# LayerNorm 2 of the first 512 tokens moved into the recurrence, the last segment woven into the first FFN chunks, one tile for the gate/up tails, LayerNorm 1's statistics issued later, and an extra output projection of half as many matmuls, in an attention-recurrence plus gated-FFN kernel

## The chip, the cores and the metric

The kernel runs on one core of one Trainium2 chip. The metric is device microseconds of one launch, the median of several runs; lower is better. A single launch is also recorded by the hardware profiler, and all views below come from such profiled executions. Engine names in them are PE (TensorE matmul), PEld (TensorE weight load), DVE (VectorE), ACT (ScalarE), POOL (GpSimd) and SP (the queue that issues DMAs); "L557" is line 557 of the kernel's file.

## The reference, cut to what matters

The sequence has S = 2048 tokens of width D = 640. Attention runs over 64 segments of 32 tokens. Each segment also sees 8 memory tokens, which are the attention output of the segment before it at its memory rows, so the segments are a chain. Then comes a gated FFN of width F = 1728.

```python
def _A_ref(x, mem0, Wq, Wk, Wv, Wo, seg_len):      # H=32 heads of 128, M=8 memory tokens
    mem, outs = mem0, []
    for s in range(n_seg):                          # 64 segments, one after the other
        h = concat([mem, x[:, s*32:(s+1)*32]])      # 40 rows
        q, k, v = h @ Wq, h @ Wk, h @ Wv
        p = softmax(mask(q @ k.T * scale))
        o = einsum('bhte,hed->btd', p @ v, Wo)
        mem = o[:, :8]                              # goes into the next segment
        outs.append(o[:, 8:])
    return concat(outs)

h  = x + _A_ref(layernorm(x), ...)                  # LN1
h2 = h + (relu(n @ W_gate) * (n @ W_up)) @ W_down   # n = layernorm(h), which is LN2
```

## The kernel before: the parts that matter

The kernel is one list of operations with read and write keys; a small dependency solver turns the keys into semaphore waits, and each engine executes its own operations in the order in which they were added. That last point decides much below: a ScalarE or VectorE operation stands behind every operation that was added for that engine before it, whether it needs it or not (in the changed kernel ScalarE once stood idle for 4.76 us in this way, and moving an operation ahead gained 8 to 10 us; both are shown below).

TensorE computes for each segment the projections (`project`, L339 and L325), transposes, scores, the memory rows' p·v (`pv_mem`), their transposes (`trans_om`) and output projection (`wo_pass`, 32 head blocks times four column groups of 32 output partitions), then the other rows' p·v (`pv_x`, L557). VectorE and ScalarE evacuate PSUM in between. The memory path, from scores to the next segment's memory rows, is the chain.

In this kernel a pass takes 32 rows of a segment, 8 of memory and 24 tokens. The last 8 tokens of each of four segments are therefore gathered in `oTe` and get an extra output projection in one pass, 16 times in all. It stands in two halves in the segments with s mod 4 = 1:

```python
    def wo_pass(src, keys, bk, halves=(0, 1)):
        for hf in halves:
            def f(pe, hf=hf):
                for hb in range(16 * hf, 16 * hf + 16):
                    w = Wo[:, head(hb // 4, hb % 4), :].rearrange("p (c g j) -> p g c j", g=4, j=32)
                    for gg in range(4):              # four column groups, 160 columns each
                        i = pe.matmul(bank(bk)[32 * gg:32 * gg + 32, 0:160], src[:, hb, :], w[:, gg],
                                      start=(hb == 0), stop=(hb == 31), ...)
# ... cut ...
    for s in range(NSEG):
        # ... projections, transposes, scores, exp_mem, cut ...
        if s == NSEG - 2:                            # W gate and W up overwrite Wq's space
            dma(Wg, ..., w=[("W", 0, 0), ("W", 0, 1), ("Wg",)])
            dma(Wu, ..., w=[("W", 0, 0), ("W", 0, 1), ("Wu",)])
        if last:
            for i in range(2):
                ln2_front(i)                         # load x and attention, add, row statistics, scale
            dma(Wd, ...)
        if units: ev[0] = units[0](); ...            # first half of the extra pass, or other extras
        if not last: pv_mem(s)
        exp_x()
        if units: ev[1] = units[1](); ev[1]()        # second half; ScalarE copies it out
        if woe: woe_store(s // 4 - 1)
        if s % 4 == 1 and ln:
            ln1_front(nb, xt, ("xt",))               # LN1: statistics and scale of the next 128 rows
        if last:
            for i in range(2):
                ln2_back(i, BQ[i])                   # transpose into xn2T
                ln2_front(i + 2)
        if not last: trans_om(s)                     # TensorE, then the VectorE copy into oT
        if s >= 1: trans_ox(s - 1, T0)
        # ... cut ...
        wo_pass(oT[par], ...)                        # needs that copy
        to_act(s + 1, ...)                           # memory rows of the next segment
        # ... stores, cut ...
        pv_x(s)
        if fin: fin()                                # Q or K of 32 further tokens: ScalarE evacuates
```

The FFN then runs over four blocks of 512 tokens: 14 chunks of gate and up (13 of 128 columns and a tail of 64), then the down products. Each down group sums all 14 chunks, so it waits for the last product into `hT`.

Of the kernel before, what the change touches and what calls it, by code (L numbers as in the profile page):

```python
# [163 lines left out]
def build_kernel(nc, A_x, A_mem0, A_Wq, A_Wk, A_Wv, A_Wo, A_seg_len, B_W_gate, B_W_up, B_W_down, out):  # L164
# [19 lines left out]
    x_ap, out_ap, mem0_ap = A_x[0], out[0], A_mem0[0]  # L184
    attn_d = nc.dram_tensor("attn_d", [S, 4, DC * 32], BF16)
# [11 lines left out]
    Wg = ffn.alloc("Wg", [128, DC, F], BF16)  # L197
    Wu = ffn.alloc("Wu", [128, DC, F], BF16)
# [3 lines left out]
    xt2 = [ffn.alloc(f"xt2_{i}", [128, D], BF16) for i in range(2)]  # L202
    at = [ffn.alloc(f"at{i}", [128, D], BF16) for i in range(2)]
    h_rows = [[ffn.alloc(f"h0_{u}", [128, D], BF16) for u in range(4)]]
    g1 = [ffn.alloc(f"g1_{i}", [128, TB], BF16) for i in range(3)]
    osb = [ffn.alloc(f"osb{i}", [128, D], BF16) for i in range(3)]
    xn2T = [ffn.alloc("xn2T0", [128, DC, TB], BF16)]
    assert ffn.off <= 2 * DC * HD * 2
    ffn.off = 2 * DC * HD * 2
    h_rows.append([ffn.alloc(f"h1_{u}", [128, D], BF16) for u in range(4)])  # L210
# [26 lines left out]
    wtoke = ar.alloc("wtoke", [128, DC, 32], BF16)  # L237
    TBf = ar.alloc("TBf", [128, DC, 32], F32)
    xt = ar.alloc("xt", [128, D], BF16)
    st = ar.alloc("st", [128, 2, 6], F32)  # L240
# [61 lines left out]
    def norm_rows(src, skey, n, dst, dkey):  # L302
        for q in range(2):
            add("dve", lambda v, q=q: v.bn_stats(st[0:n, q, :], src[0:n, q * 320:(q + 1) * 320]), r=[skey],  # L304
                w=[("st", q)])
        add("dve", lambda v: v.bn_aggr(mv[0:n, :], st[0:n, :, :]), r=[("st", 0), ("st", 1)], w=[("mv",)])
        add("act", lambda a: a.activation(lv[0:n, :], mv[0:n, 1:2], ACTF.Ln, bias=eps[0:n, 0:1], scale=1.0),
            r=[("mv",), ("eps",)], w=[("lv",)])
        add("act", lambda a: a.activation(rs[0:n, :], lv[0:n, :], ACTF.Exp, scale=-0.5), r=[("lv",)], w=[("rs",)])
        add("dve", lambda v: v.tensor_scalar(dst[0:n, :], src[0:n, :], mv[0:n, 0:1], rs[0:n, 0:1], ALU.subtract,  # L310
                                             ALU.mult), r=[skey, ("mv",), ("rs",)], w=[dkey])
# [103 lines left out]
    def ln1_front(b, buf, key):  # L415
        t0, n = (0, 64) if b < 0 else (64 + 128 * b, min(128, S - 64 - 128 * b))
        norm_rows(buf, key, n, buf, key)
# [34 lines left out]
    def to_act(s, wkey, src):  # L452
# [4 lines left out]
            w=[("act", b % 2, j, "m")])  # L457

# [78 lines left out]

    def wo_rows(bk, dst, dkey, eng):
        copy_op(eng, dst[:].rearrange("p c j -> p (c j)"), bank(bk)[:, 0:160], [B(bk)], [dkey])
# [43 lines left out]
    def attn_keys(i):  # L583
        ks = []
        for s in range(4 * i, 4 * i + 4):
            ks += [("attn", 32 * s, g) for g in range(4)] + [("attn", 32 * s + RID, g) for g in range(4)]
        return ks

    def ln2_front(i):
        par, u, e = (i // 4) % 2, i % 4, i % 2  # L590
        x2, xk, a2, ak = xt2[e], ("xt2", e), at[e], ("at", e)
        dma(x2[:, :], x_ap[128 * i:128 * i + 128, :], r=[("Wdone", 1)], w=[xk])
        dma(a2[:, :], attn_d[128 * i:128 * i + 128, :, :].rearrange("t g f -> t (g f)"), r=attn_keys(i) + [("Wdone", 1)],
            w=[ak])
        h = h_rows[par][u]
        hk = ("h", par, u)
        add("dve", lambda v: v.tensor_tensor(ap(h, 0, [[128, 5], [32, 4], [1, 32]]),
                                             ap(x2, 0, [[128, 5], [32, 4], [1, 32]]),
                                             ap(a2, 0, [[32, 5], [160, 4], [1, 32]]), ALU.add),
            r=[xk, ak], w=[hk])  # L600
        norm_rows(h, hk, 128, x2, xk)

    def ln2_back(i, bk):
        par, u, e = (i // 4) % 2, i % 4, i % 2
        transpose_rows(xt2[e], ("xt2", e), 128, bk)
# [21 lines left out]
    ln1_front(-1, xt, ("xt",))  # L627
    ln1_trans(-1, xt, ("xt",), P0)
    ln1_back(-1, P0)
    ln1_front(0, x0, ("oTe", 0))  # L630
# [38 lines left out]

    def extra_units(s):  # L670
# [23 lines left out]
    oTe_keys = [("oTe", q) for q in range(4)]  # L694

    def woe_units():
        def first():
            wo_pass(oTe, oTe_keys, BQ[0], (0,))
            return None

        def second():
            wo_pass(oTe, oTe_keys, BQ[0], (1,))
            return lambda: wo_rows(BQ[0], wtoke, ("wtoke",), "act")
        return [first, second]

    def woe_store(b):
        for j in range(4):
            for g in range(4):
                t0 = 32 * (4 * b + j) + RID
                dma(attn_d[t0:t0 + M, g, :], wtoke[32 * g + M * j:32 * g + M * j + M, :, :].rearrange("p c j -> p (c j)"),  # L710
                    r=[("wtoke",)], w=[("attn", t0, g)])

    fullr = (FC - 1) * 128
    for s in range(NSEG):
# [5 lines left out]
        if s % 4 == 0 and ln:  # L720
            ln1_load(nb, xt, ("xt",))
        if s > 0:
# [4 lines left out]
            to_tok(BQ[1], 1, "dve")  # L727
            if not last:
# [15 lines left out]
        if not last:  # L744
            exp_mem()
# [3 lines left out]
        if s == NSEG - 2:  # L749
            dma(Wg[:, :, :], B_W_gate.rearrange("(c p) f -> p c f", p=128), w=[("W", 0, 0), ("W", 0, 1), ("Wg",)])  # L750
            dma(Wu[:, :, :], B_W_up.rearrange("(c p) f -> p c f", p=128), w=[("W", 0, 0), ("W", 0, 1), ("Wu",)])
        if last:
            for i in range(2):
                ln2_front(i)
            dma(Wd[:, 0:FC - 1, :], B_W_down[0:fullr, :].rearrange("(j p) d -> p j d", p=128),
                w=[("W", 1, 0), ("W", 1, 1), ("Wd", 0)])
            dma(Wd[0:FR, FC - 1, :], B_W_down[fullr:F, :], w=[("W", 1, 0), ("W", 1, 1), ("Wd", 1)])
        units, fin = extra_units(s)
        woe = s % 4 == 1 and s >= 5
        if woe:  # L760
            units = woe_units()
        ev = [None, None]
        if units:
            ev[0] = units[0]()
            if ev[0]:
                ev[0]()
        if not last:
            pv_mem(s)
        exp_x()
        if units:  # L770
            ev[1] = units[1]()
            ev[1]()
        if woe:
            woe_store(s // 4 - 1)
        if s % 4 == 1 and ln:
            ln1_front(nb, xt, ("xt",))
        if last:
            for i in range(2):
                ln2_back(i, BQ[i])
                ln2_front(i + 2)  # L780
        if not last:
            trans_om(s)
        if s >= 1:
            trans_ox(s - 1, T0)
        if s % 4 == 2 and ln:
            ln1_trans(nb, xt, ("xt",), BQ[1])
            ln1_back(nb, BQ[1])
        wo_pass(oT[par], [("oT", par, "m"), ("oT", par, "x")], T1)
        if not last:
            to_act(s + 1, B(T1), bank(T1)[:, 0:160])  # L790
# [3 lines left out]
        pv_x(s)  # L794
        if fin:
# [4 lines left out]
    for i in (2, 3):  # L800
        ln2_back(i, BT[i % 2])
    tail = [lambda: trans_ox(NSEG - 1, BT[0])]
    for s in (NSEG - 2, NSEG - 1):
        par = s % 2

        def wo_last(s=s, par=par):
            wo_pass(oT[par], [("oT", par, "m"), ("oT", par, "x")], BT[par])
            wo_rows(BT[par], wtok[par], ("wtok", par), "dve")
            store_attn(wtok[par], ("wtok", par), M, 32 * s, RID)
        tail.append(wo_last)  # L810

    def woe_last():
        wo_pass(oTe, oTe_keys, BT[0])
        wo_rows(BT[0], wtoke, ("wtoke",), "act")
        woe_store(NSEG // 4 - 1)
    tail.append(woe_last)
# [3 lines left out]
    def gate_up(b, j):  # L820
        par = b % 2
        nf = 128 if j < FC - 1 else FR
# [5 lines left out]
        def mk(w, bk):  # L828
            def f(pe):
                for c in range(DC):  # L830
                    ins = pe.matmul(bank(bk)[0:nf, :], w[:, c, j * 128:j * 128 + nf], xn2T[par][:, c, :],  # L831
                                    start=(c == 0), stop=(c == DC - 1))
                return ins
            return f
        add("pe", mk(Wg, bg), r=xk + [("Wg",)], w=[B(bg)])
        add("pe", mk(Wu, bu), r=xk + [("Wu",)], w=[B(bu)])
        add("act", lambda a: a.activation(g1[gi][0:nf, :], bank(bg)[0:nf, :], ACTF.Relu), r=[B(bg)],
            w=[("g1", gi)])
        add("dve", lambda v: v.tensor_tensor(hT[par][0:nf, j, :], g1[gi][0:nf, :], bank(bu)[0:nf, :], ALU.mult),
            r=[B(bu), ("g1", gi)], w=[("hT", par, j)])  # L840

    def down(b, u):
# [3 lines left out]
        hk = [("hT", par, j) for j in range(FC)]  # L846
        for hf in range(2):
            bk = BD[hf]

            def f(pe, hf=hf, bk=bk):  # L850
                for j in range(FC):
                    nf = 128 if j < FC - 1 else FR
                    i = pe.matmul(bank(bk)[:, 0:320], hT[par][0:nf, j, u * 128:(u + 1) * 128],  # L853
                                  Wd[0:nf, j, hf * 320:(hf + 1) * 320], start=(j == 0), stop=(j == FC - 1))
                return i
            add("pe", f, r=hk + [("Wd", 0), ("Wd", 1)], w=[B(bk)])
            add("dve", lambda v, hf=hf, bk=bk: v.tensor_tensor(osb[o][:, hf * 320:(hf + 1) * 320], bank(bk)[:, 0:320],
                                                            h_rows[par][u][:, hf * 320:(hf + 1) * 320], ALU.add),
# [3 lines left out]

    for b in range(NBLK):
        for j in range(FC):
            gate_up(b, j)
            if b + 1 < NBLK and j % 3 == 1 and j < 12:
                ln2_front(4 * (b + 1) + j // 3)
            if b + 1 < NBLK and j % 3 == 0 and j:
# [68 lines left out]
```

## Time and profile before

| | before |
|---|---|
| time, median of 3 runs | 1328.67 us (1323.97 to 1329.94) |
| span of the profiled execution | 1312.9 us |
| TensorE busy | 1174.1 us, 89% |
| recurrence, first to last memory-attention exp (ScalarE's exp of the memory rows' scores, one in each segment but the last) | 993.7 us |
| turn, last memory-attention exp to first up matmul | 43.5 us |
| first FFN block, first up matmul to its first down matmul | 46.7 us |
| the rest of the FFN | 166.9 us |

Four lines of the profile's page of before. The first is the span, the second the busy time of each engine with its share and its instructions, the third the queue that the page calls "instruction" (packets, MB, share of 16 engines), the fourth the shares of the chain that ended last.

```profile
span 1312.9 us, 66508 instructions
...
PE 1174.1 (89%) x32475; PEld 681.2 (52%) x29795; DVE 549.7 (42%) x1420; ACT 484.4 (37%) x894; POOL 4.1 (0%) x21
...
q8 instruction: 244, 4.00, 1.2%
...
PE 86%; issue 4%; DVE 3%; DMA 3%; ACT 1%; SPq 1%; POOL 0%; DVEq 0%; POOLq 0%; ACTq 0%
```

TensorE is busy 89% of the time and makes up 86% of the chain, so the kernel is bound by TensorE work in nearly all places; what is not TensorE lies in few. The instruction queue has 244 packets of 16 KiB.

The windows view of before cuts the span at the stages of the table above. Columns: from and to; length; busy us of each engine with its instructions; then the granted TensorE clock, the DMA engines' busy share and GB/s.

```profile
core 0: us, PE busy (x) PEld busy (x) DVE busy (x) ACT busy (x) POOL busy (x), PEclk, DMA share, GB/s
62.10:1055.80 993.70, 923.95 (x29943) 552.22 (x27463) 441.13 (x1187) 416.62 (x761) 0.00 (x0) 1.00 0.09 21
1055.80:1099.30 43.50, 19.89 (x596) 13.46 (x577) 15.65 (x41) 9.43 (x22) 0.00 (x0) 0.78 0.57 197
1099.30:1146.00 46.70, 41.10 (x549) 22.02 (x548) 18.23 (x37) 13.72 (x28) 0.00 (x0) 0.91 0.09 25
1146.00:1312.90 166.90, 161.35 (x908) 84.35 (x908) 60.19 (x114) 33.28 (x66) 0.00 (x0) 1.00 0.10 32
```

In the turn TensorE is busy for 19.9 of 43.5 us and the granted clock is 0.78. Within it, between 1075 and 1085 us, the windows view gives 2.75 us busy of 10 and a clock of 0.50. In finer windows TensorE has no instruction from 1070 to 1080 us, and the clock is 0.50 in all of them from 1074 to 1086 us.

The chain through that turn, from the chain of waits of before (start, us, what):

```profile
1058.46 8.83 DMA Wg<-in_B_W_gate_dram
...
1070.14 7.29 DMA at_56<-attn_d
...
1095.07 0.73 PE ps L316 x5
...
1097.17 3.92 PE ps L831 x10
```

The W gate load ends at 1067.3, and the W up load was issued behind it. Then attention rows arrive from DRAM, four groups of LN2 follow one after the other on VectorE, the last of them is transposed at 1095.1, and only at 1097.2 does the first gate matmul start.

The wait table of before for TensorE. Columns after the colon: us in total, times, longest.

```profile
PE ps L557 <- issue: 28.6, 30, 2.0
PE ps L533 <- DVE oT_101 L374: 18.7, 15, 1.8
...
PE ps L533 <- issue: 9.9, 12, 1.3
...
PE ps L853 <- DVE hT_74 L839: 1.5, 2, 0.8
```

"issue" is idle time for which the profile shows no cause. The second line is the wait of the memory rows' output projection for the VectorE copy into oT, 1.2 us on average in the 15 segments in which LN1 runs (1, 5, ... 57; all but the first of them also have an extra pass). The last line, with its twin for the other buffer (also 1.5 us), is the wait of the down products for hT, 0.78 us per block.

The timeline of before shows where the second line comes from, in segment 17 (start, us, engine, line, what; in brackets the idle time before it and what ended it):

```profile
330.98 1.30 PE L533 MATMUL ps<-Wo,oTe 128*32 128x160 bf16 x64
...
332.32 1.29 PE L533 MATMUL ps<-Wo,oTe 128*32 128x160 bf16 x64
...
333.29 0.88 DVE L304 BATCH_NORM_STATS2 st<-xt 128x6 f32<-128x320 bf16 x2
...
335.09 0.45 DVE L310 TENSOR_SCALAR xt<-xt,mv,rs 128x640 bf16<-128x640 bf16 x1 [0.67 <-ACT rs L309]
335.45 0.28 DVE L374 COPY oT_101<-ps 128x256 bf16<-128x256 bf16 x1
...
335.79 2.40 PE L533 MATMUL ps<-Wo,oT_101 128*32 128x160 bf16 x128 [1.51 <-DVE oT_101 L374]
```

The two half passes over oTe take 1.30 and 1.29 us. VectorE starts LN1's row statistics at 333.3, waits for ScalarE's reciprocal root, scales at 335.1, and only then copies into oT_101, for which TensorE has stood still for 1.5 us.

### The profile page before, as it was taken

The page shows a single profiled execution, that of the slowest core. Times are in us where ns is not written, and L with a number is a line of the kernel's source. Part 1 is how long each engine was busy: PE and PEld are TensorE (multiplying, and loading weights), DVE is VectorE, ACT ScalarE, POOL GpSimd, SP SyncE. Part 2 cuts the span into 40 slices and gives each one's busy share as a digit, 9 for nine tenths or more (in the row PEclk, how much of TensorE's full clock was granted, in tenths as well). Part 3 has the DMA queues.
Part 4 walks back from the last instruction along what each step waited for, and adds up shares of the span by engine and source line. Part 5 has one row for each costly group of instructions (what it writes and reads, how often), then busy time and mean ns, then how long its engine had stood idle before and what let it go on. Part 6 is the DMA issues. An engine that isn't in the chain of part 4 may idle for free.

```text
span 1312.9 us, 66508 instructions
## 1 busy us (share of the span) xinstructions
PE 1174.1 (89%) x32475; PEld 681.2 (52%) x29795; DVE 549.7 (42%) x1420; ACT 484.4 (37%) x894; POOL 4.1 (0%) x21
## 2 busy tenths in 40 slices
PE   1789999999998999999999999899989857899998
PEld 0245555555555555555555555555555525355454
DVE  2244444444444444444444444444444333433522
ACT  0234344444443434444444434343434322221311
POOL 1000000000000000000000000000000000000000
PEclk9999999999999999999999999999999988899999
DMA  9701010000000001010010000100000061110100
GB/s 367 285 22 25 19 24 19 24 19 23 19 23 19 23 20 24 20 24 22 20 23 23 20 23 20 24 21 22 21 19 18 19 227 38 32 61 22 40 21 20
DMA packets 44691, 57.53 MB, mean 44 GB/s; under 512 B 19264, under 2 KB 33280, under 8 KB 44416
## 3 DMA queue, kind: packets, MB, share of 16 engines
q1 hardware_dynamic: 40384, 42.80, 11.4%
q10 hardware_dynamic: 4032, 10.49, 2.1%
q8 instruction: 244, 4.00, 1.2%
q14 instruction: 31, 0.25, 0.1%
HBM read 35.48 MB, written 5.24 MB: 31 GB/s over the span
## 4 chain that ended last, share of the span: by engine, by line
PE 86%; issue 4%; DVE 3%; DMA 3%; ACT 1%; SPq 1%; POOL 0%; DVEq 0%; POOLq 0%; ACTq 0%
PE ps L339 30%; PE ps L533 14%; PE ps L325 11%; PE ps L831 9%; PE ps L358 6%; PE ps L853 5%; PE ps L557 3%; PE ps L475 2%; PE ps L366 2%; DMA W<-in_A_Wk_dram 2%; PE ps L508 1%; SPq L300 1%; PE ps L316 1%; DVE st L304 1%; PE ps L520 1%
## 5 line engine op out<-in xcount | busy, mean ns | idle before, releaser
L339 PE MATMUL ps<-W,act_r_81 128*32 128x512 bf16 x2660 | 222.1, 385 | 11.2 <-DMA W<-in_A_Wk_dram 8.5
L339 PE MATMUL ps<-W,act_r_80 128*32 128x512 bf16 x2540 | 208.7, 380 | 2.9 <-issue 2.8
L339 PEld LDWEIGHTS ps<-W,act_r_81 128*32 128x32 bf16 x2660 | 73.7, 97 | 149.8 <-issue 95.6
L325 PE MATMUL ps<-W,act_r_81 128*32 128x512 bf16 x1380 | 140.8, 389 | 0.9 <-issue 0.9
L339 PEld LDWEIGHTS ps<-W,act_r_80 128*32 128x32 bf16 x2540 | 70.1, 96 | 128.6 <-issue 85.2
L325 PE MATMUL ps<-W,act_r_80 128*32 128x512 bf16 x1300 | 129.6, 379 | 0.3 <-issue 0.3
L372 ACT ACTIVATE tok_84<-ps 128x512 bf16<-128x512 f32 x67 | 40.1, 598 | 170.6 <-PE ps L325 170.6
L533 PE MATMUL ps<-Wo,oT_101 128*32 128x160 bf16 x4224 | 81.1, 235 | 19.8 <-DVE oT_101 L374 18.7
L372 ACT ACTIVATE tok_86<-ps 128x512 bf16<-128x512 f32 x94 | 56.2, 598 | 104.6 <-PE ps L325 103.6
L533 PEld LDWEIGHTS ps<-Wo,oT_101 128*32 128x32 bf16 x4224 | 73.8, 98 | 25.5 <-DVE oT_101 L374 21.3
L374 DVE CAST tok_85<-ps 128x512 bf16<-128x512 f32 x67 | 46.4, 692 | 96.9 <-PE ps L325 96.9
L374 DVE CAST tok_87<-ps 128x512 bf16<-128x512 f32 x64 | 44.3, 692 | 94.8 <-PE ps L325 94.8
L568 DVE TENSOR_TENSOR ox<-ps,rx 128x512 bf16<-128x512 f32 x128 | 82.5, 686 | 2.2
L372 ACT ACTIVATE Kr<-ps 128x768 bf16<-128x768 bf16 (+3 forms) x89 | 68.0, 775 | 34.9 <-DVE KmT L374 17.8
L533 PE MATMUL ps<-Wo,oT_100 128*32 128x160 bf16 x4224 | 79.7, 233 | 0.8 <-issue 0.4
L372 ACT ACTIVATE Qr<-ps 128x512 bf16<-128x512 bf16 (+3 forms) x110 | 68.9, 659 | 17.9 <-PE ps L358 16.7
L533 PEld LDWEIGHTS ps<-Wo,oT_100 128*32 128x32 bf16 x4224 | 72.6, 97 | 5.1 <-issue 1.0
L339 PE MATMUL ps<-W,act_e_82 128*32 128x512 bf16 x960 | 61.0, 380 | 0.0
L455 DVE STREAM_TRANSPOSE TBf<-ps 128x160 f32<-128x160 f32 x64 | 22.4, 350 | 88.3 <-PE ps L533 88.3
L339 PE MATMUL ps<-W,act_e_83 128*32 128x512 bf16 x840 | 53.4, 380 | 0.0
L533 PE MATMUL ps<-Wo,oTe 128*32 128x160 bf16 x2048 | 43.8, 233 | 8.6 <-issue 8.6
L374 DVE COPY KmT<-ps 128x256 bf16<-128x256 bf16 x64 | 18.7, 292 | 60.7 <-PE ps L358 60.7
(178 smaller groups left out, 1696.3 us busy)
## 6 DMA issues: line engine op xcount, KB each, us to landing
attn_d<-wtoke SPq DMA_DIRECT2D x256, 2.5 KB
W<-in_A_Wk_dram ACTq DMA_DIRECT2D x1, 2560.0 KB
W<-in_A_Wq_dram ACTq DMA_DIRECT2D x1, 2560.0 KB
W<-in_A_Wv_dram ACTq DMA_DIRECT2D x1, 2560.0 KB
Wo<-in_A_Wo_dram ACTq DMA_DIRECT2D x1, 2560.0 KB
W<-in_A_Wk_dram SPq DMA_DIRECT2D x1, 2560.0 KB
W<-in_A_Wq_dram SPq DMA_DIRECT2D x1, 2560.0 KB
W<-in_A_Wv_dram SPq DMA_DIRECT2D x1, 2560.0 KB
```

The costliest lines, as they stand in the source:

```text
L325: return pe.add_instruction(mybir.InstMatmult(name=nc.get_next_instruction_name(), engine=mybir.EngineType.PE, ins=[pe.lower_ap(rhs), pe.l ...
L339: ins = pe.matmul(*a, start=(c == 0), stop=(c == DC - 1), skip_group_check=True)
L358: ins = pe.matmul(bank_bf(b)[:, k * 128:(k + 1) * 128], t[:, (k % 4) * 128:(k % 4 + 1) * 128], ident[:, :], is_transpose=True)
L366: i = pe.matmul(bank_bf(b)[:, k * 128:(k + 1) * 128], t[:, k // 2, k % 2, :], ident[:, :], is_transpose=True)
L372: add("act", lambda a: a.activation(dst, src, ACTF.Copy), r=r, w=w)
L374: add("dve", lambda v: v.tensor_copy(dst, src), r=r, w=w)
L475: i = pe.matmul(o, lh, Qr[:, h, q, :], start=True, stop=True, skip_group_check=True)
L533: i = pe.matmul(bank(bk)[32 * gg:32 * gg + 32, 0:160], src[:, hb, :], w[:, gg], start=(hb == 0), stop=(hb == 31), skip_group_check=True)
L557: i = pe.matmul(bank(P0 + g)[32 * c:32 * c + 32, 129 * kh:129 * kh + 129], Px[32 * g:32 * g + n, 256 * a + 32 * k:256 * a + 32 * k + 32], ...
L568: add("dve", lambda v, kh=kh: v.tensor_tensor(ox[:, :, kh, :], src[:, :, kh, 0:128], ap(rx, kh, [[2, 4], [0, 128]]), ALU.mult), r=[B(P0 + ...
L831: ins = pe.matmul(bank(bk)[0:nf, :], w[:, c, j * 128:j * 128 + nf], xn2T[par][:, c, :], start=(c == 0), stop=(c == DC - 1))
L853: i = pe.matmul(bank(bk)[:, 0:320], hT[par][0:nf, j, u * 128:(u + 1) * 128], Wd[0:nf, j, hf * 320:(hf + 1) * 320], start=(j == 0), stop=(j ...
```

## The change

Its intent, part by part:

1. LN2 of block 0 (tokens 0 to 511) is done in four "early" places of the recurrence (segments 31, 35, 39, 43 and the ones after them). The sum h and the transposed normalized rows go to DRAM and are loaded back at the turn.
2. The last segment's other-rows p·v and the last output projections are woven into the first four gate/up chunks.
3. The 64-wide tails of gate and up share one 128-wide tile (`Wgu`), so each block has five matmuls fewer; the down sum is issued in two pieces so that only the second waits for the last two chunks.
4. LN1's row statistics are split from the scaling: statistics after `pv_x`, scaling in the next segment.
5. The extra output projection becomes "2x2": two halves of the heads times two halves of the columns. A half pass is 32 matmuls of 320 columns in place of 64 of 160. Each half of the heads is summed into two of the four column groups, and the two partial sums are added afterwards (`woe_sum`).

The diff, cut to its core:

```diff
-        if last:
-            for i in range(2):
-                ln2_front(i)
-            dma(Wd[:, 0:FC - 1, :], ...)
+    def woe_pass(bk, kg):
+        def f(pe):
+            for i in range(16):
+                for dg in range(2):
+                    q = 2 * kg + dg
+                    hb = 16 * kg + i
+                    w = Wo[:, head(hb // 4, hb % 4), :].rearrange("p (c g j) -> p g c j", g=4, j=32)
+                    ins = pe.matmul(bank(bk)[32 * q:32 * q + 32, 0:320], oTe[:, hb, :], w[:, 2 * dg:2 * dg + 2],
+                                    start=(i == 0), stop=(i == 15), skip_group_check=True)
... cut ...
+    def load_gate_up():
+        free = [("W", 0, 0), ("W", 0, 1)]
+        dma(xn2T[0][:, :, :], xn2_d[:, :, :], ...)
+        for n, (t, src) in enumerate(((Wg, B_W_gate), (Wu, B_W_up))):
+            dma(t[:, :, :], src...[:, :, 0:FM], w=free + [(("Wg", "Wu")[n],)])
+            dma(Wgu[:, :, n * FR:(n + 1) * FR], src...[:, :, FM:F], w=free + [("Wgu", n)])
... cut ...
+    EARLY = (31, 35, 39, 43)
+        if s % 4 == 3 and e2 is not None:
+            dma(xt[:, :], x_ap[128 * e2:128 * e2 + 128, :], w=[("xt",)])
+            load_attn(at, e2, [], ("at",))
... cut ...
+            if s % 4 == 2 and ln:
+                row_scale(xt, ("xt",), n_rows(nb), xt, ("xt",))
+            if e2b is not None:
+                row_scale(xt, ("xt",), 128, at, ("at",))
... cut ...
         if woe:
-            woe_store(s // 4 - 1)
-        if s % 4 == 1 and ln:
-            ln1_front(nb, xt, ("xt",))
+            woe_pass(BQ[0], 1)
+        trans_om(s)
         if s >= 1:
             trans_ox(s - 1, T0)
+        if woe:
+            woe_sum(BQ[0])
+            woe_store(s // 4 - 1)
... cut ...
         pv_x(s)
+        if s % 4 == 1 and ln:
+            row_stats(xt, ("xt",), n_rows(nb))
+        if s % 4 == 3 and e2 is not None:
+            add_attn(xt[:, :], xt, at, [("xt",), ("at",)], [("xt",)])
+            dma(h_d[128 * e2:128 * e2 + 128, :], xt[:, :], r=[("xt",)], w=[("h_d", e2)])
+            row_stats(xt, ("xt",), 128)
         if fin:
             fin()
... cut: gate/up tail in one tile ...
-                for j in range(FC):
+            for lo, hi in ((0, FC - 2), (FC - 2, FC)):
+                    for j in range(lo, hi):
... cut ...
+    gate_up(0, 0)
+    pv_x(s)
+    gate_up(0, 1)
+    trans_ox(s, P0)
+    wo_pass(oT[(s - 1) % 2], oT_keys((s - 1) % 2), P1)
... cut: two more chunks with wo_pass and woe_pass between them ...
```

## The prediction

> What bounds it now. The page gives TensorE 89% busy and 86% of the chain. Where it does not work:
> - The turn from recurrence to FFN. In timeline and windows TensorE is nearly idle from 1068.7 us (last scores) to 1097.2 (first gate matmul). The chain there: W gate load (issued 1058.5, 8.8 us), W up load waiting for it (1067.3), loads of x and attention for LN2, four LN2 row groups (2.7 us of VectorE each), transposes. Another gap of 4.8 us stands at 1122. The granted clock is 0.50 in 1075-1085[...].
> - In the wait table TensorE waits 18.7 us, 15 times, for the VectorE copy into oT_101: segments with the extra Wo pass, where LN1's row statistics stand ahead of that copy.
> - About 48 us of "issue" gaps. In the timeline they end about 2.4 us after a 16 KiB packet of the instruction queue starts (244 packets, 4.00 MB). [...] I estimate a block can't take less than about 3.2 us. Extra-Wo segments are densest and stall most.
>
> Changes, costed.
> 1. LN2 of block 0 leaves the turn; the first gate matmul waits only for W up. The loads stay serialized by shared keys: xn2T (about 2 us) goes ahead of W gate, a tail load (about 3 us) between W gate and W up. Estimate: W up lands near 1081 on before's axis, instead of a start at 1097: -16. [...]
> 2. Weaving: the last segment's pv joins block 0 (+0.7); the 4.8 us gap and its cold clock go (-6.7).
> 3. Tails in one tile: five 216 ns matmuls fewer per block, -4.3 over four. Splitting the down sum removes the 0.78 us wait for hT per block: -3.1.
> 4. Row statistics after pv: the 18.7 us wait goes.
> 5. 2x2 extra Wo: a half pass used four column groups (64 matmuls of 160 columns, 1.1 us). Now 32 of 320 columns use two groups at a time, so I expect 2.2 us: +2.1 per pass, 16 passes, but 128 instructions fewer each. Respacing before's instructions with the 3.2 us block estimate, items 4 and 5 together give about -6 over the recurrence (item 4 alone -14, part coming back as fetch stalls). The pass in the tail adds +2.
> 6. Early LN2: four transposes and fillers, +1.6.
>
> Sum: -16 -6.7 +2.7 -4.3 -3.1 -6 +1.6 = about -32 us.
>
> Predicted: 1295 us (from 1328.67), eight in ten 1278 to 1307. Faster by over 2%: 0.72; within 2%: 0.26; slower: 0.02.
>
> Right or wrong in the profile: first gate matmul near 1075 us of the span, released by the W up load; oTe matmuls about 70 ns start to start, half passes 2.2 us; no wait for oT_101; issue gaps in extra-Wo segments down from about 1.3 us to some tenths; down starts without a gap; no gap over 2 us in block 0.
>
> What would make it wrong: half passes running near 1.1 us after all (then about 1266); waits moving to another VectorE or ScalarE operation; early-LN2 segments stalling; serialized loads landing later, or ScalarE held by a late store of wtok while W down loads.

Two passages on how the chip works and a remark on the clock at the start are cut above, because they rested on more than this case's traces. No term of the sum goes with them: it stays at about -32 us. What its terms take from before's trace:

- The 216 ns are the median distance from start to start of gate and up matmuls (five in 1.08 us at 1119.7 us).
- Of the 6.7 us, 4.8 are the gap, which ends at 1126.9 us. The other 1.9 stand for the clock: it is at half from 1124.3 to 1131.1 us, 6.8 us, of which TensorE works for the last 4.2.
- The times for loading xn2T and the tail were estimates, with no source given.
- The 1.1 us of a half pass run from the first start to the last, where my 1.30 us elsewhere run to the last end. That it doubles with two groups was an estimate (measured below: 2.35 us, and 1.28 again in e1).
- A "block" is 256 TensorE instructions, the spacing at which the issue gaps stand (below). The 3.2 us for it are an estimate; the packets of the instruction queue start at least 3.28 us apart in before.

## The result, and the profile after

| | before | after |
|---|---|---|
| time, median | 1327.02 us (4 runs, 1323.97 to 1329.94) | 1290.64 us (4 runs, 1288.8 to 1291.8) |
| ratio of fast runs | | 0.9725, 95% interval 0.9696 to 0.9753 |
| span of the profiled execution | 1312.9 us | 1287.1 us |

A ratio is the mean time of one kernel's fast runs over the mean of the other's in the same rounds, so it is not quite the ratio of the two medians. The change is faster by 2.75%, and the time lies 4 us from the predicted one. The profiled execution of before was its fastest (1314.6 us, where the timed runs took 1324 us or more), so the profiles differ by 25.8 us and the timed runs by about 36. The profile is used here for where the difference lies, and the timed runs for how large it is.

The page of after, the same parts:

```profile
span 1287.1 us, 64249 instructions
...
PE 1192.4 (93%) x31431; PEld 689.6 (54%) x28751; DVE 553.9 (43%) x1434; ACT 484.3 (38%) x896; POOL 4.1 (0%) x21
...
PE 89%; DMA 4%; issue 3%; DVE 1%; SPq 1%; ACT 1%; POOL 0%; POOLq 0%; ACTq 0%
```

TensorE's busy share rose from 89 to 93% and its busy time by 18 us, although it executes 1044 matmuls fewer (31431 against 32475). Busy time is no gain here: part of it is the slower half pass, as shown below.

The windows of after, cut at the same events, with the columns as before:

```profile
61.40:1057.20 995.80, 949.26 (x29003) 565.78 (x26523) 454.14 (x1222) 421.70 (x773) 0.00 (x0) 1.00 0.10 24
1057.20:1081.90 24.70, 16.08 (x511) 9.69 (x492) 6.29 (x18) 5.77 (x11) 0.00 (x0) 0.92 0.61 211
1081.90:1126.00 44.10, 42.52 (x543) 22.23 (x544) 18.01 (x37) 11.77 (x27) 0.00 (x0) 0.93 0.33 102
1126.00:1287.10 161.10, 157.61 (x896) 82.89 (x893) 60.96 (x116) 33.77 (x69) 0.00 (x0) 1.00 0.10 33
```

| stretch | before, us | after, us | difference | predicted |
|---|---|---|---|---|
| up to the first memory-attention exp | 62.1 | 61.4 | -0.7 | 0 |
| recurrence | 993.7 | 995.8 | +2.1 | -4.4 (items 4, 5 and 6) |
| turn | 43.5 | 24.7 | -18.8 | |
| first FFN block | 46.7 | 44.1 | -2.6 | |
| turn and first block together | 90.2 | 68.8 | -21.4 | about -21.9 |
| rest of the FFN | 166.9 | 161.1 | -5.8 | about -5.6 |

The predicted -21.9 is -16 - 6.7 + 0.7 + 2 from items 1, 2 and 5, less one quarter of item 3 (1.85); the -5.6 is the other three quarters of item 3's 7.4. So the sums after the recurrence came out within half a microsecond of what was costed, and the recurrence did not: it was to shorten by 4.4 us and lengthened by 2.1 in these two profiles. The split between turn and first block is less exact than their sum. Costed like the sum, the turn was to lose about 16 us and lost 18.8, because the first gate chunk ran while W up was still loading; the first block was to lose about 5.9 and lost 2.6, because TensorE then waited for W up and the clock was at half for 6.8 us from 1081.3, nearly all of it inside the block.

The chain of waits of after through the turn:

```profile
1060.76 10.24 DMA Wg<-in_B_W_gate_dram
...
1071.01 2.13 DMA Wgu<-in_B_W_gate_dram
...
1073.16 8.62 DMA Wu<-in_B_W_up_dram
...
1081.92 2.29 PE ps L855 x5
```

LN2 is gone from it. The loads are what was predicted: W gate, the tail tile, W up, one behind the other because they share write keys. The first chunk's five gate matmuls ran at 1075.9, directly behind TensorE's own work of the last segment; then TensorE waited 4.8 us for W up until 1081.9.

The wait table of after for TensorE:

```profile
PE ps L577 <- issue: 28.2, 26, 1.6
...
PE ps L345 <- ACT Qr L378: 7.0, 4, 1.9
PE ps L855 <- DMA Wu<-in_B_W_up_dram: 4.8, 1, 4.8
...
PE ps L540 <- DVE oT_99 L380: 0.4, 1, 0.4
```

The wait for oT went from 18.7 us to 0.4, and the wait for hT is absent from the table. New is the second line: 7.0 us in four places, where a projection waits for ScalarE's evacuation into Qr. The early LN2 has four places.

The timeline of after at one of the two new things, the extra pass in segment 17:

```profile
329.52 2.08 PE L553 MATMUL ps<-Wo,oTe 128*32 128x320 bf16 x28
...
331.92 2.20 PE L553 MATMUL ps<-Wo,oTe 128*32 128x320 bf16 x30
...
334.17 0.61 PE L372 MATMUL ps<-ident,ox 128*128 128x128 bf16 x8
334.72 1.50 PE L540 MATMUL ps<-Wo,oT_100 128*32 128x160 bf16 x76
```

The timeline merges only records that follow each other, so each half pass is split, but its length is plain: 28 matmuls in 2.08 us, 30 in 2.20. A whole half pass has a median of 2.35 us from its first start to its last end, against 1.30 before. The output projection that follows starts without a wait.

And at the other, segments 43 to 44, the last early LN2:

```profile
761.06 0.89 DVE L308 BATCH_NORM_STATS2 st<-xt 128x6 f32<-128x320 bf16 x2
...
762.22 0.29 ACT L311 ACTIVATE lv<-mv,eps 128x1 f32<-128x1 f32 x1 [4.76 <-DVE mv L310]
...
762.66 1.00 ACT L378 ACTIVATE Qr<-ps 128x1024 bf16<-128x1024 bf16 x1
...
763.72 0.40 PE L345 MATMUL ps<-W,act_r_80 128*32 128x512 bf16 x4 [1.93 <-ACT Qr L378]
```

VectorE does the statistics of the early LN2 at 761.1. ScalarE stands idle for 4.76 us, because its next operation in order is the logarithm of these statistics. The evacuation into Qr, whose source had been in PSUM since 759.5, comes behind it at 762.7. TensorE's next projection needs the bank that this evacuation frees and waits 1.93 us.

To see the recurrence by kind, I summed the times of segments, measured in each trace from one memory-attention exp to the next, by s mod 4 (r1 has the extra pass; r3 has the early LN2's sum and statistics and the start of the segment after it). "Fetch gaps" is my name for TensorE idle time over 0.1 us that stands directly ahead of the first instruction of a block of 256 TensorE instructions; the first of the two columns counts those in r1 segments, the second those of the whole recurrence. The first segment is left out of r0.

| us, summed | r0 | r1 | r2 | r3 | fetch gaps in r1 | fetch gaps, recurrence |
|---|---|---|---|---|---|---|
| before | 228.2 | 278.1 | 239.8 | 231.9 | 21.4 | 46.8 |
| after | 227.9 | 269.8 | 241.4 | 240.7 | 9.1 | 35.1 |

The kinds tell two stories: r1, where items 4 and 5 act, gained 8.3 us (predicted 6), and r3, where the early LN2 acts, lost 8.8 us (predicted 1.6 for it in all). Single profiles are good for a few microseconds here: 3.7 of the 8.3 us stand in segment 61, which has no LN1 and took 20.1 us in before, with the clock at half for 3.4 us of it, and 16.4 in after. The 1.6 us more in r2 are not assigned: r2 varies by as much between the experiments' kernels that share its code.

Why "fetch": the gaps that the profile calls "issue" stand at TensorE instruction numbers, matmuls and weight loads counted together, that are equal modulo 256 (all 55 over 0.1 us in before, 40 of 41 in after), and end about 2.4 us after a 16 KiB packet of the instruction queue started (2.2 to 3.1 in before). The 46.8 us of before are 3.6% of its span. The traces list 62,505 TensorE instructions in before and 60,423 in after, 244 and 236 times 256, and the pages have as many packets of that queue, 244 and 236. So I read a packet as the instructions of one block; what a packet holds is not in the trace. Matched in order, so that each late block (one with a fetch gap ahead of it) follows its packet by those 2.4 us, the packet for the next block starts 0.8 us (median) after a block has begun, and never more than 3.3 us before that. By this reading about one block is fetched ahead in this trace, and no two packets start less than 3.28 us apart.

### The profile page after: what moved, and what is told of

Same layout as the page of the kernel before. It is cut to its first block, busy times and chain, and to the rows that moved or that the text cites. A ratio compares the mean times of both kernels' runs of the same rounds, so it can differ in the third digit from the quotient of the medians.

```text
span 1287.1 us, 64249 instructions
## 1 busy us (share of the span) xinstructions
PE 1192.4 (93%) x31431; PEld 689.6 (54%) x28751; DVE 553.9 (43%) x1434; ACT 484.3 (38%) x896; POOL 4.1 (0%) x21
## 3 DMA queue, kind: packets, MB, share of 16 engines
q1 hardware_dynamic: 43520, 45.41, 12.4%
## 4 chain that ended last, share of the span: by engine, by line
PE 89%; DMA 4%; issue 3%; DVE 1%; SPq 1%; ACT 1%; POOL 0%; POOLq 0%; ACTq 0%
PE ps L345 30%; PE ps L540 11%; PE ps L331 11%; PE ps L855 8%; PE ps L364 6%; PE ps L883 5%; PE ps L553 5%; PE ps L577 4%; PE ps L482 3%; PE ps L372 2%; DMA W<-in_A_Wk_dram 2%; PE ps L515 1%; PE ps L527 1%; SPq L304 1%; PE ps L322 1%
## 5 line engine op out<-in xcount | busy, mean ns | idle before, releaser
L378 ACT ACTIVATE Qr<-ps 128x512 bf16<-128x512 bf16 (+3 forms) x110 | 68.8, 658 | 14.6 <-PE ps L364 13.5
L553 PE MATMUL ps<-Wo,oTe 128*32 128x320 bf16 x1024 | 73.0, 299 | 0.0
L553 PEld LDWEIGHTS ps<-Wo,oTe 128*32 128x32 bf16 x1024 | 50.2, 97 | 14.5 <-issue 0.4
L311 ACT ACTIVATE lv<-mv,eps 128x1 f32<-128x1 f32 (+1 forms) x33 | 9.7, 295 | 115.8 <-DVE mv L310 115.8
```

Of the source, the lines that this page charges most:

```text
L378: add("act", lambda a: a.activation(dst, src, ACTF.Copy), r=r, w=w)
L553: ins = pe.matmul(bank(bk)[32 * q:32 * q + 32, 0:320], oTe[:, hb, :], w[:, 2 * dg:2 * dg + 2], start=(i == 0), stop=(i == 15), skip_group_ ...
```

## The experiments

Two questions were open. Which part of the change made r3 longer? And what did items 4 and 5 do singly, where I had said that 4 gains 14 us and 5 gives 8 of them back? The rival was that the 2x2 pass pays for itself, through fewer instructions to fetch. Where variants of the changed kernel are compared with it, I use medians: its own were 1290.64 and, run again as a control, 1289.75 us, while before's varied from 1319.4 to 1327.0 and moves the ratios with it.

### The extra pass over four column groups (e1_four_groups)

The same 32 matmuls of 320 columns in a half pass, with the order changed so that consecutive ones go to all four column groups instead of two.

```diff
-            for i in range(16):
-                for dg in range(2):
-                    q = 2 * kg + dg
-                    hb = 16 * kg + i
+            for i, q in [(i, q) for i in range(8 * half, 8 * half + 8) for q in range(4)]:
+                    kg, dg = q // 2, q % 2
+                    hb = 16 * kg + i
```

> The changed kernel, but each half of the extra Wo pass takes 8 heads of every quarter and cycles over all four column groups (32 matmuls of 320 columns, as many as now). Theory (two groups at a time cost a factor of two): a half pass falls from about 2.1 us to 1.1 us, 16 passes give 16 x 2 = 32 us less TensorE time; some comes back as instruction-fetch gaps, so 22 to 32 us faster than the changed kernel (about 1260 to 1268). Rival (the pass is held by instruction supply, so its time per instruction does not matter): fetch gaps take it all back, within 5 us of the changed kernel (1286 to 1293).

Measured: 1272.52 us (1267.56 to 1276.77), ratio 0.9610 (0.9585 to 0.9635), 18 us below the changed kernel. Its timeline at segment 17's extra pass:

```profile
323.55 1.28 PE L552 MATMUL ps<-Wo,oTe 128*32 128x320 bf16 x32
...
324.87 1.27 PE L552 MATMUL ps<-Wo,oTe 128*32 128x320 bf16 x32
```

A half pass takes 1.28 us at the median against 2.35: only the order of the column groups differs, so the factor of 1.84 is the number of groups in use. Over 32 half passes the sum fell from 74.6 to 41.2 us, which is 33 us, and the time fell by 18. One part of the remainder is visible: the fetch gaps in r1 rose from 9.1 to 14.9 us. My reading, not tested by itself, is that the same instructions now have less time to arrive. The direction was as expected, and the size was below the expected 22 to 32.

### The old extra pass, the rest of the change kept (e2_old_extra_wo)

```diff
-            woe_pass(BQ[0], 0)
+            wo_pass(oTe, oTe_keys, BQ[0], (0,))
...
-            woe_pass(BQ[0], 1)
+            wo_pass(oTe, oTe_keys, BQ[0], (1,))
```

The sum of the two partial results becomes one ScalarE copy, 16 stores replace 8, and both stand ahead of `trans_om` again, as before.

> The changed kernel with the extra Wo pass as before (128 matmuls of 160 columns, 16 stores), all else kept. Theory (the prediction's step 5): the 2x2 pass costs more than its fewer instructions save once the VectorE wait is gone, so this is about 8 us faster than the changed kernel (about 1283), with fetch gaps up by some 15 us. Rival (the 2x2 pass pays by itself): 10 us or more slower (1300 or more).

Measured: 1301.17 us (1299.42 to 1304.13), ratio 0.9818 (0.9793 to 0.9843), about 11 us slower than the changed kernel. My prediction had this kernel faster than the changed one; the rival was right. Its wait table:

```profile
PE ps L577 <- issue: 38.2, 32, 1.9
PE ps L540 <- issue: 19.5, 23, 1.5
...
PE ps L540 <- DVE oT L380: 0.4, 1, 0.4
```

The wait for oT is as short as in the changed kernel (0.4 us), and the half passes are short again (1.30 us). But the issue lines grew from 28.2 and 1.3 us to 38.2 and 19.5, and the fetch gaps in r1 from 9.1 to 36.8 us. In segments 9 and 13, a late block that follows a late block takes 3.7 to 4.0 us; the whole recurrence has 22 such pairs, all in r1 segments, at 3.5 to 4.3 us, 3.7 at the median. My estimate had been 3.2, which is about the shortest distance of two packets and not what such a pair takes.

### The evacuation ahead of the early LN2 (e3_fin_first)

Only the order within ScalarE's and VectorE's lists changes: the Q evacuation of the early segments is issued before the early LN2's sum and statistics.

```diff
         if s % 4 == 3 and e2 is not None:
+            if fin:
+                fin()
+                fin = None
             add_attn(xt[:, :], xt, at, [("xt",), ("at",)], [("xt",)])
```

> The changed kernel with the evacuation of the extra query transposes issued ahead of the early LN2 statistics in the four segments 31, 35, 39, 43. Theory (ScalarE waits in order for VectorE's statistics, and TensorE for ScalarE's copy into Qr, 7.0 us in 4 waits): those waits vanish, 6 to 7 us faster than the changed kernel (about 1284). Rival (the early segments are long for other reasons, the instruction fetch or the loads): at most 2 us faster and another wait in its place.

Measured: 1280.66 us (1280.52 to 1282.43), ratio 0.9664 (0.9641 to 0.9686), 10 us below the changed kernel by medians and 8 by the ratios. The wait for Qr is absent from its wait table, r3 fell from 240.7 to 235.0 us, and the recurrence took 988.7 us. So the wait for the Q evacuation was the cost, and its cause was the order, as no operation was removed. The drop of r3 (5.7 us) is nearly the 7.0 us of the wait; the timed gain is larger than either by a few microseconds, and I did not locate these.

### Loads that don't wait for each other (e4_load_keys)

```diff
-        free = [("W", 0, 0), ("W", 0, 1)]
+        free = [("Wdone", 0)]
...
-            dma(t[:, :, :], ..., w=free + [(("Wg", "Wu")[n],)])
+            dma(t[:, :, :], ..., r=free, w=[(("Wg", "Wu")[n],)])
```

The loads still wait until the last Q projection has read the old weights, as a read of its key, but no longer for each other. The W down loads were treated likewise.

> The changed kernel with the gate, up and down weight loads no longer waiting for each other (they wait for the projections that read the old weights, no more). Theory (serialized loads set when the first up matmul starts, 1081.9 us): W up lands about 4 us earlier, the 4.8 us wait shrinks under 1.5 us and the half-clock matmuls after it go, so 4 to 6 us faster (about 1285). Rival (the loads are bound by bandwidth and the turn by the order of the work): under 1.5 us faster.

Measured: 1284.58 us (1284.2 to 1287.88), ratio 0.9696 (0.9671 to 0.9720), 6 us below the changed kernel, about as expected. In its profile the turn took 21.7 us (24.7) and the first block 40.9 (44.1). W gate and W up now load at the same time and both land about 19.6 us after the last memory-attention exp, where W up alone had landed after 24.2; the price is that W gate lands later (in the changed kernel its load ends at 1071.0 us, 13.8 after that exp), so TensorE idles 3.8 us ahead of the first gate chunk instead of 4.8 us within it. The half clock did not go as expected: it lasts 6.8 us there in both kernels.

### The three together (e5_best)

The edits of e1, e3 and e4.

> Four column groups, the early evacuation of the queries, and the unchained weight loads together (the edits of e1, e3 and e4). If the three act in different stretches they add: ratios to before of 0.961, then 0.006 and 0.004 less, so about 0.951 (1261 us) and faster than any run so far. If the shorter extra Wo pass or the shorter waits come back as instruction-fetch gaps, 0.956 or more.

Measured: 1254.73 us (1253.3 to 1258.13), ratio 0.9512 (0.9492 to 0.9533), the fastest kernel, 5% below before and 36 us below the changed one. The three edits by themselves had given 18, 10 and 6 us by medians, so they add.

### The old place of LN1's statistics (e6_stats_old)

The changed kernel with item 4 undone: statistics and scaling of LN1 stand ahead of the copy into oT again.

```diff
+        if s % 4 == 1 and ln:
+            row_stats(xt, ("xt",), n_rows(nb))
+            row_scale(xt, ("xt",), n_rows(nb), xt, ("xt",))
         trans_om(s)
...
-        if s % 4 == 1 and ln:
-            row_stats(xt, ("xt",), n_rows(nb))
```

> The changed kernel with LN1's statistics and scaling back where they were, ahead of the attention copy of segments 1, 5, 9, ... Theory A (the prediction's step 4: the 18.7 us wait was worth about its length): the wait for oT returns, 14 to 19 us slower than the changed kernel (1305 to 1310). Theory B (the half pass of 2.35 us, 1.05 us longer than before, covers most of what VectorE does there, and the rest is time in which the next instruction block is fetched): wait for oT under 8 us, 0 to 6 us slower (1290 to 1297).

Measured: 1299.95 us (1299.27 to 1304.23), ratio 0.9857 (0.9836 to 0.9878), 10 us slower than the changed kernel. The wait for oT is back, 11.0 us in 16 places, r1 grew by 12.4 us (282.2), and its fetch gaps stayed (8.4 against 9.1). The result lies between the two ranges. The wait in its table:

```profile
PE ps L540 <- DVE oT L380: 11.0, 16, 1.8
```

The wait is shorter than in before (18.7) because the longer half pass (2.35 us in the changed kernel against 1.30) keeps TensorE busy while VectorE works.

### Four groups and the old place of the statistics (e7_four_stats_old)

The edits of e1 and e6.

> e1 (four column groups) with LN1's statistics back where they were. Here the half pass is 1.28 us again, as in the kernel before, so the wait for oT should return at about 18 us in 15 waits. If a wait and a fetch gap are the same time spent twice, the fetch gaps of these segments fall by two thirds or more of it and the kernel is 2 to 8 us slower than e1 (1274 to 1281); if they add, 15 to 18 us slower (1287 to 1291).

Measured: 1286.09 us (1282.57 to 1290.63), ratio 0.9751 (0.9728 to 0.9774), 13.6 us slower than e1. The wait for oT is 23.8 us in 16 places, the fetch gaps in r1 fell from 14.9 to 8.2 us, and r1 grew by 19.2 us over e1.

```profile
PE ps L540 <- DVE oT L380: 23.8, 16, 1.9
```

The time lies between the two expected ranges, nearer to the one for costs that add. With the pass short and its instructions few, the statistics' old place costs most, and only part of the wait (the 6.7 us by which the fetch gaps fell, of 23.8) is time that the fetch would have taken anyway. So here the two costs nearly add, and do not hide each other.

### The changed kernel again (e8_after_again)

No edit; a control.

> The changed kernel once more, unedited, as the control on this chip: the ratio to before should come out within 0.9696 to 0.9753, as at first.

Measured: 1289.75 us (1287.09 to 1290.99), ratio 0.9768 (0.9744 to 0.9792). The time agrees with the first within 1 us; the ratio is 0.4 points above the first (0.9725) and a little above what I had expected, because before itself ran at a median of 1319.39 us. Ratios of different calls should not be compared more closely than that. The kinds of segments repeat: r1 269.2 and r3 242.8 us, against 269.8 and 240.7.

### Two groups with narrow matmuls (e9_narrow_two_groups)

The changed kernel's two groups at a time, with each matmul of 320 columns cut into two of 160: as many instructions as the old pass, at the 2x2 pass's pace.

```diff
-                    ins = pe.matmul(bank(bk)[32 * q:32 * q + 32, 0:320], oTe[:, hb, :], w[:, 2 * dg:2 * dg + 2], ...)
+                    for c2 in range(2):
+                        ins = pe.matmul(bank(bk)[32 * q:32 * q + 32, 160 * c2:160 * c2 + 160], oTe[:, hb, :],
+                                        w[:, 2 * dg + c2], start=(i == 0 and c2 == 0), ...)
```

> The changed kernel with each 320-column matmul of the extra Wo pass split into two of 160 columns in the same column group: 128 instructions more per pass, the same two groups at a time, half pass still about 2.3 us. With the changed kernel (64 matmuls, two groups), e1 (64, four) and e2 (128, four) it completes the square. Theory (instruction count is what e2 paid for: a block of 256 instructions needs 3.7 us or so when the one before it was late): fetch gaps of the segments with the pass rise by 8 to 20 us over the changed kernel, 8 to 20 us slower (1299 to 1311). Rival (e2 was slower for another reason, such as its 16 stores or ScalarE copy): within 3 us of the changed kernel.

Measured: 1299.14 us (1293.06 to 1305.82, six runs), ratio 0.9845 (0.9816 to 0.9874), 9 us slower than the changed kernel, at the bottom of the expected range. A half pass takes 2.40 us as in the changed kernel (2.35), so the pace doesn't depend on the number of instructions. Segments r1 grew by 8.4 us. I can account for 2.9 us of that as fetch gaps and 2.0 us as longer half passes in total; about 3.5 us I could not locate. So that the instruction count by itself costs about 9 us here is shown; that all of it is fetch is not. Against e2, which has as many instructions over four groups, this kernel is no slower (1299.14 against 1301.17 us), although each of its half passes is 1.1 us longer: e2's fetch gaps in r1 are 36.8 us against 12.0 here. With 128 matmuls in the pass the faster pace is worth nothing, and with 64 it is worth 18 us (e1).

### The old pass and the old place of the statistics (e10_old_wo_stats_old)

Items 4 and 5 both undone, all else of the change kept.

> e2 (old extra Wo pass) with LN1's statistics back where they were: the kernel before's segments, with early LN2 and the new tail. In e2 the wait for oT was gone but the fetch gaps of the segments with the pass had risen from 21.4 to 36.8 us. If with the long pass the wait and the fetch are the same time spent twice, bringing the wait back costs 0 to 5 us over e2 (0.982 to 0.986 of before) and those fetch gaps fall to about 21 us. If they add, as e6 and e7 did with the short pass, 14 to 19 us (0.992 to 0.996).

Measured: 1298.56 us (1297.27 to 1302.92), ratio 0.9849 (0.9823 to 0.9875), so by medians no slower than e2 (1301.17), which has the statistics moved (by the ratios, which come from different calls, 0.3% slower). Its wait table, against that of e2 above:

```profile
PE ps L577 <- issue: 31.5, 31, 2.0
PE ps L540 <- DVE oT L380: 18.4, 16, 1.8
...
PE ps L540 <- issue: 10.7, 12, 1.4
```

The wait for oT is back at 18.4 us, and the fetch gaps in r1 are down from 36.8 to 21.5: with the old pass, TensorE spends about the same time either waiting for VectorE (18.0 us more) or in the fetch gaps (15.3 us less). Moving the statistics only changed the name of the wait. This was expected and is what the run showed.

### One down sum instead of two (e11_no_split)

The changed kernel without the split of item 3.

```diff
-            for lo, hi in ((0, FC - 2), (FC - 2, FC)):
+            for lo, hi in ((0, FC),):
```

> The changed kernel with each down sum as one instruction group again. Prediction's step 3: the 0.78 us wait for hT before each block's down matmuls comes back, about 0.8 us more from one block's first down matmul to the next's (47.24 us now), 3.1 us in all. Rival (the wait would be short anyway, since the half-height last chunk is alone): under 0.3 us per block.

Measured, one run: 1300.47 us, of unknown state; its time is not used. In its profile the distance from one block's first down matmul to the next one's is 48.85 us, against 47.24 in the changed kernel and 49.29 in before. TensorE waits for hT 6.2 us in four places, 1.55 each, twice what I had expected (0.8). My reading of the code, not tested by itself, is that the merged tail has no separate up matmuls, which used to run while ScalarE and VectorE finished the product before, so that merged tail and split belong together. The table's line (its releaser is the product into hT):

```profile
PE ps L883 <- DVE hT L870: 6.2, 4, 1.6
```

The tail tile alone is worth about 0.4 us per block (49.29 - 48.85), both together 2.05.

### The runs of items 4 and 5 in one table

All kernels in it have the rest of the change. Medians in us, with the sum of r1 segments in brackets.

| extra pass, per half | LN1 statistics ahead of the oT copy | statistics after p·v |
|---|---|---|
| 64 matmuls, four groups (old) | 1298.56 (278.7), e10 | 1301.17 (276.1), e2 |
| 32 matmuls, two groups (2x2) | 1299.95 (282.2), e6 | 1290.64 and 1289.75 (269.8, 269.2), changed and e8 |
| 32 matmuls, four groups | 1286.09 (266.6), e7 | 1272.52 (247.4), e1 |

From left to right in the first row: nothing gained, because the wait and the fetch gaps take each other's place (18.4 and 21.5 us in e10, 0.4 and 36.8 in e2). From the first row to the second in the left column: nothing gained either, but not because one wait hid the other. Both fell there, to 11.0 and 8.4 us, and the slower pace took it back: the 32 half passes grew from 43.3 to 74.6 us in sum, idle time within them left out. Both at once: about 8 us. The third row keeps the pace, and there each step pays by itself, 12.5 us for fewer instructions (e10 to e7) and 13.6 us more for the moved statistics (e7 to e1).

## Why the prediction was right or wrong

**The total was right, within 4 us, and two errors in it cancelled in part.** The time lies inside the range, and "faster by over 2%" had the highest chance. The sum of the prediction was -32 us; the timed runs gave -36 and the pair of profiles -25.8, since the profiled execution of before was a fast one. Where the 10 us between these two measures lie is not known, as before's slower executions have no profile here (for their clock, see the end of this section); the terms below are held against the profiles.

**Items 1, 2 and 3: right in sum, and mostly in mechanism.** Turn and first block together measured -21.4 us against about -21.9, the rest of the FFN -5.8 against -5.6. That the first sum is so near is in part luck, as its two stretches missed by about 3 us in opposite directions. The down sums start without a wait for hT. No gap over 2 us stands in block 0 once W up is there; counted from its first gate matmul, it has the one of 4.8 us. One sign was stated too simply: the first gate matmul was to start near 1075 us, released by W up. It started at 1075.9, but behind TensorE's own preceding work and not behind a load; W up released the first up matmul, at 1081.9, after a wait of 4.8 us. That 1075 was met is chance, since the recurrence did not get shorter. The load that I had put at 1081 on before's axis landed there: the first up matmul came 24.7 us after the last memory-attention exp, where 25.2 had been costed. Of item 3, the split is worth more than I had costed and the tail less: e11 shows 1.6 and 0.4 us per block, where I had 0.78 and 1.1.

**The warned risk of a late store holding ScalarE was real and cost nothing.** In the woven part ScalarE stood 12.1 us for a store of wtok while W down loaded, and TensorE lost 0.25 us by it.

**Item 6 was wrong: "Early LN2: four transposes and fillers, +1.6".** The step counted only TensorE's added work. Measured were 8.8 us in r3. The added statistics stand ahead of an evacuation in ScalarE's order, and TensorE needs that evacuation. Moving nothing but the order (e3) took the wait away and 8 to 10 us of the time, and left r3 at 235.0 us, 3.1 above before. I had listed "early-LN2 segments stalling" among what could go wrong, but costed none of it.

**Items 4 and 5 together: near (-6 predicted, -8.3 measured in r1), but each by itself wrong.** The prediction had "item 4 alone -14" and, by the difference, +8 for the 2x2 pass. The chip gives for item 4 alone -2.0 us in r1 (e2 against before), or +2.6 in the timed runs (e2 against e10), and for the 2x2 pass -6.3 in r1 and -11 in the timed runs (e2 to the changed kernel). That the sum of the two came near is luck: two misses of opposite sign. The failing term of the sum is "the 3.2 us block estimate": with 3.2 us for a block of 256 instructions, the densest segments could use the time that item 4 freed. A late block behind a late block took 3.5 to 4.3 us in e2, and over its 22 pairs the excess above 3.2 adds up to 13 us, an estimate from that trace and about the 12 us by which item 4 alone was missed. So the freed time was spent waiting for instructions (fetch gaps in r1 from 21.4 to 36.8 us), and fewer instructions were worth more than the slower pace cost.

**The two-groups term was right.** "I expect 2.2 us" per half pass; the median was 2.35, and e1 shows with the same instructions in another order (1.28 us) that the number of groups in use is the reason. What I did not ask is whether the order was free to change: it was, and that alone was worth 18 us.

**"Issue gaps in extra-Wo segments down from about 1.3 us to some tenths": half right.** Spread over 15 or 16 such segments, the fetch gaps went from about 1.4 us each (21.4 in sum) to 0.6 (9.1).

**Still open.** The fetch is read from the spacing of the gaps and the packets of the queue, and its dependence on the instruction count from e2, e9 and e10; no run delayed or sped up the fetch itself. 3.5 us of e9 and several of e1's and e3's gains are not located, and nor is what makes before's executions differ by up to 15 us. One lead for the last: in the 29 timed executions of before that list their granted clock, it is 0.979 to 0.987 and the time falls as it rises (correlation -0.62), while the profiled one had 0.987. Their mean of 0.9825 would be about 11 us more at half clock, so up to 5 or 6 of the 10 us between the two measures, by this estimate. No run shows whether the lower clock is a cause there or follows from idle time.

## What to carry to other kernels

- When a wait stands where the engine is also short of instructions, removing the wait alone can change only its name (nothing gained, 1298.56 to 1301.17 us, e10 to e2), and a fix of the other can be eaten by what it costs (the slower pace, 1298.56 to 1299.95 us, e10 to e6). Cost such fixes as a pair, and test them in a table of kernels that changes one thing at a time.
- Work that is "off the critical path" still takes a place in an engine's order: before adding it, ask which evacuation stands behind it, since exchanging two calls was worth 8 to 10 us here.
- When small matmuls go to separate column groups, let consecutive ones cycle over all groups (32 matmuls of 320 columns took 1.28 us over four groups, 2.35 over two), and count instructions as well as columns: here the four groups gained 18 us with 64 matmuls in the pass (e1 against the changed kernel) and nothing with 128 (e2 at 1301.17 us, e9 at 1299.14).
